# Products of probabilities and v, chunk by chunk on 64 rows and 32 columns of the array

## The chip, the cores and the metric

The kernel runs on one core of a Trainium2 chip. Its time is the device time of one execution in microseconds, given as the median of several; shorter is better. The core has TensorE (PE, matmuls into PSUM), VectorE (DVE), ScalarE (ACT), GpSimd (POOL) and SyncE (SP, which issues DMAs). They run side by side and wait for each other by semaphores.

## The reference

Two steps: attention by chunks, and a gated feed-forward network over all tokens. q, k and v are 4 x 8 heads x 768 tokens x 64, in float32. Each chunk of 32 queries sees 64 keys: 8 memory keys, 16 to its left, its own 32 and 8 to its right.

```
for c in range(nc):                                   # 24 chunks of 32
    k_full = concat([mem_k, k[l_start:r_end]])        # up to 64 keys
    v_full = concat([mem_v, v[l_start:r_end]])
    scores = scale * q_c @ k_full.T
    a = exp(scores - max(scores))
    a = a / (sum(a) + 1e-09)
    out[c] = a @ v_full
...
xn = x / sqrt(mean(x * x) + 1e-06) * rms_g            # x: 3072 tokens x 512
g, val = xn @ w_gate, xn @ w_val                      # 512 -> 1536
return (silu(g) * val) @ w_out                        # 1536 -> 512
```

## The kernel before

The 3072 tokens are 8 blocks of 384 tokens. A block's attention is 4 units of work, 32 in all, each two heads by 384 tokens, that is 12 chunks for each head. The feed-forward part of a block goes over 12 slices of 128 hidden columns; each slice has 12 matmuls `pg` (gate), 12 `pv` (value), both at L561, and 9 `po` (output) at L599. They work in a shortened float32 (fp32r) on values split into a high and a low part, so that each product is three matmuls.

Units 0 to 7 (two blocks) run at the start, in an order written out by hand as a string of tokens, while weights are still loaded and split. The other 24 units, of blocks 2 to 7, are put between the feed-forward matmuls of the block before: a generator puts the steps of its four units into the gaps between groups of matmuls, in six visits and one more for the norm. In visit n these are `stage_p` of unit n-1, `stage_s` of unit n, then `stage_o` and `stage_r` of unit n-2, and the steps after them. On TensorE everything of this later part stays in the order of the program (`on_pe`); the order of the other engines comes from a scheduler.

The steps of a unit that matter here:

- `stage_s` (L318) multiplies q and k: 12 matmuls in plain float32, one for each chunk, with 64 output rows (two heads x 32 queries) and 64 keys. The two heads' q lie block-diagonally in `qb` (`qp` in the late units), 128 x 64, so that one matmul over 128 rows (two heads x 64) does both heads.
- the maximum (L330), the difference (L336) and the exponential (L341) make `pe`.
- `stage_p` (L348) transposes `pe` into `pT`, three 128 x 128 blocks. In `pT` the partitions are keys: 64 of one chunk, 64 of the next.
- `stage_ch` (L227) copies `pT` into `pt` (late: a part of the tile `qp`), where each pair of chunks stands block-diagonally: rows 0 to 63 only in the columns of the first chunk of the pair (index cp = 0), rows 64 to 127 only in those of the second. The other places were set to zero once.
- `stage_o` (L368) multiplies `pt` by v. `vw` (late: `kv`) holds for each pair of chunks the 64 keys of one chunk on rows 0 to 63 and those of the other on rows 64 to 127, with a column of ones at the end that sums the probabilities. A matmul over 128 rows and 64 columns does a pair of chunks of one head: 65 moving columns, 12 matmuls a unit, into one bank of PSUM, `o`. The index par (0 or 1) puts the output on the partitions from 0 or from 64, and so on the left or right half of the array's columns.
- `stage_ra`, `stage_rb`, `stage_rc` (L382, L386, L391) divide by the sums into `x`.

`x` is then normed (L398, L411, L421), transposed into `xT` (L440) and split.

Of the kernel before, what the change touches and what calls it, by code (L numbers as in the profile page):

```python
# [17 lines left out]
B, H, S, D = 4, 8, 768, 64  # L18
NM = 8
CH = 32  # L20
# [47 lines left out]
def tile_kernel(ctx: ExitStack, tc: tile.TileContext, q, k, v, mem_k, mem_v,  # L68
                w_gate, w_val, w_out, rms_g, out):
    nc = tc.nc  # L70
# [35 lines left out]
    def on_pe(ins):  # L106
        if pinned:
            tc.keep_in_program_order(ins)

    def psum_a(name):  # L110
        return psa.tile([P, 512], F32, name=name, tag="at")

    def psum_m(tag, name):
        return psm.tile([P, 512], F32, name=name, tag=tag)
# [19 lines left out]
    def which(u):  # L134

        return 1 + u % 2 if u < NE else 0
# [223 lines left out]
    def stage_o(u):  # L360
        d = st[u]
        pt = pts[which(u)]
        o = psum_a(f"o{u}") if u >= NG else psum_m(f"o{1 + u % 2}", f"o{u}")
        for i in range(NT):
            for hh in range(2):
                for par in range(2):
                    c0 = (2 * i + hh) * (D + 1)
                    on_pe(nc.tensor.matmul(o[64 * par:64 * par + 64, c0:c0 + D + 1],  # L368
                                     lhsT=pt[:, i, 2 * par + hh].rearrange("p c q -> p (c q)"),
                                     rhs=d["v"][:, 2 * i + par, hh, :], start=True, stop=True))  # L370
        d["o"] = o

    def stage_r(u, x):
# [306 lines left out]
    for e in range(2):  # L680
        r = slice(64 * e, 64 * e + 64)
# [6 lines left out]
    def attn_visits(blk, x):  # L688


        us = list(range(blk * NG, (blk + 1) * NG))
        for n in range(NG + 2):
            with tc.high_priority():
                if 1 <= n <= NG:
                    stage_p(us[n - 1])
                if n < NG:
                    u = us[n]
                    stage_s(u)
                if n >= 2:
                    stage_o(us[n - 2])  # L700
                    stage_r(us[n - 2], x)
                if n < NG:
                    stage_m(u)
                    stage_e(u)
                if 1 <= n <= NG:
                    stage_c(us[n - 1])
                if n < NG and u + 1 < len(units):
                    stage_t(u + 1)
            if n >= 2 and us[n - 2] + 1 < len(units):
                load_v(us[n - 2] + 1)  # L710
            if n < NG and u + 2 < len(units):
                load_qk(u + 2)
            yield
        with tc.high_priority():
            stage_n(x)
        yield
# [75 lines left out]
    def tok_o(n):  # L792
# [12 lines left out]
        S=stage_s, M=stage_ma, a=stage_mb, E=stage_e, P=stage_p,  # L805
        C=lambda n, e="a": stage_ch(n, 0, e), m=lambda n, e="a": stage_ch(n, 1, e),
        O=stage_o, X=stage_ra, x=stage_rb, u=tok_u,

        N=tok_N, e=tok_e, Y=tok_Y, y=tok_y, z=tok_z, r=tok_r, A=tok_A, B=tok_B, D=tok_D,
# [119 lines left out]
```

## Time and profile before

| | before |
|---|---|
| median of 3 runs | 733.04 us (732.32 to 733.74) |
| the profiled execution, its own time | 731.54 us |
| its span on the core | 729.8 us |
| mean granted TensorE clock | 0.995 |
| matmul records of `o` in late units | 576 |
| matmul records of `s` in late units | 576 |

A line of the groups gives the line of the kernel, the engine and operation, the output and inputs by the program's names, the shape, how many, busy time and the mean of one in ns, and the idle time of the engine ahead of them with its cause. A matmul's shape reads rows*columns of the array that are in use, then partitions x elements of the moving operand. PE is TensorE's matmuls, PEld its weight loads. A line of the chain of waits gives the start, the length and what the program's end hung on in that time.

### The profile page before, as it was taken

To read this page: it belongs to the slowest core of one execution; us is meant where nothing else is said; L and a number is where in the kernel's file an instruction comes from. 1 tells how busy PE (TensorE), PEld (TensorE's weight loads), DVE (VectorE), ACT (ScalarE), POOL (GpSimd) and SP (SyncE) were. 2 spreads that over 40 slices of the span, in tenths; PEclk is the share of its full clock that TensorE was granted. 3 is DMA by queue.
4 is the path that set the end of the run, shared out by engine and by line. 5 is a ranking of instruction groups with operands and counts; after the bars stand their busy time and mean duration, and the time that the engine had idled before them with its cause. 6 is when DMAs were issued, how large, how long until landed. Compare 5 with 4: busy or idle time off the path is not lost.

```text
span 729.8 us, 13052 instructions
## 1 busy us (share of the span) xinstructions
PE 715.1 (98%) x5136; PEld 656.6 (90%) x5136; DVE 380.0 (52%) x725; ACT 287.8 (39%) x600; POOL 36.4 (5%) x143
## 2 busy tenths in 40 slices
PE   8889999999999999999999999999999999999997
PEld 7778999999989999899999999989998999999996
DVE  4888999865645443444535353445434543332222
ACT  4899676643452323422333232432234222341112
POOL 3300000001000000000000000000000000000000
PEclk8999999999999999999999999999999999999999
DMA  8994563414412320122212123021311210010001
GB/s 173 203 259 141 173 202 116 132 37 102 85 37 68 55 50 22 62 46 42 43 38 66 23 45 61 20 66 31 66 29 34 64 32 20 20 44 0 1 1 43
DMA packets 143173, 50.20 MB, mean 69 GB/s; under 512 B 126984, under 2 KB 134536, under 8 KB 143112
## 3 DMA queue, kind: packets, MB, share of 16 engines
q1 hardware_dynamic: 139832, 44.49, 26.6%
q10 hardware_dynamic: 3280, 4.88, 1.8%
q8 instruction: 40, 0.66, 0.4%
q14 instruction: 21, 0.17, 0.1%
HBM read 43.06 MB, written 6.29 MB: 68 GB/s over the span
## 4 chain that ended last, share of the span: by engine, by line
PE 92%; ACT 3%; DMA 3%; DVE 1%; issue 0%; POOL 0%; ACTq 0%; SPq 0%; POOLq 0%
PE pv L561 28%; PE po L599 28%; PE pg L561 27%; PE s L318 3%; PE o L368 3%; PE xT L440 1%; PE pT L348 1%; DMA ws<-in_moe_w_val_dram 1%; DMA memV<-in_mem_v_dram 1%; DMA vw<-in_v_dram 1%; ACT junk L398 0%; ACT ws L508 0%; ACT pt L227 0%; DMA kv<-in_v_dram 0%; ACT qb L227 0%
## 5 line engine op out<-in xcount | busy, mean ns | idle before, releaser
L561 PE MATMUL pv<-xh,wh_v 128*128 128x384 f32 x384 | 132.8, 346 | 0.0
L561 PE MATMUL pg<-xh,wh_g 128*128 128x384 f32 x384 | 129.7, 338 | 0.7 <-DVE t L572 0.7
L561 PE MATMUL pv<-xh,wl_v 128*128 128x384 f32 x384 | 129.5, 337 | 0.6 <-DVE wl_v L532 0.6
L561 PE MATMUL pg<-xh,wl_g 128*128 128x384 f32 x384 | 129.5, 337 | 0.0
L561 PE MATMUL pg<-xl,wh_g 128*128 128x384 f32 x384 | 129.3, 337 | 0.0
L561 PE MATMUL pv<-xl,wh_v 128*128 128x384 f32 x384 | 129.3, 337 | 0.0
L572 DVE SCALAR_TENSOR_TENSOR t<-t,pg 128x384 f32<-128x384 f32 x96 | 53.1, 553 | 138.6 <-ACT t L568 138.5
L227 ACT CAST hh<-t 128x384 fp32r<-128x384 f32 x95 | 48.7, 512 | 174.9 <-PE po L599 165.3
L599 PE MATMUL po<-wh_o,hh 128*128 128x512 f32 x285 | 113.8, 399 | 0.3
L599 PE MATMUL po<-wh_o,hl 128*128 128x512 f32 x285 | 113.1, 397 | 0.0
L599 PE MATMUL po<-wl_o,hh 128*128 128x512 f32 x285 | 112.1, 393 | 0.0
L584 DVE TENSOR_TENSOR hl<-t,hh 128x384 fp32r<-128x384 f32 x95 | 52.9, 557 | 100.7 <-ACT hh L227 95.7
L568 ACT ACTIVATE t<-pg 128x384 f32<-128x384 f32 x96 | 47.2, 492 | 135.9 <-PE pg L561 130.8
L575 DVE TENSOR_TENSOR t<-t,pv 128x384 f32<-128x384 f32 x95 | 52.5, 552 | 64.9 <-PE pv L561 64.4
L561 PEld LDWEIGHTS pg<-xh,wh_g 128*128 128x128 f32 x384 | 72.1, 188 | 4.4 <-DVE t L572 0.9
L561 PEld LDWEIGHTS pg<-xl,wh_g 128*128 128x128 f32 x384 | 72.1, 188 | 3.6
L561 PEld LDWEIGHTS pv<-xh,wh_v 128*128 128x128 f32 x384 | 72.1, 188 | 2.4
L561 PEld LDWEIGHTS pv<-xh,wl_v 128*128 128x128 f32 x384 | 72.2, 188 | 0.9 <-DVE wl_v L532 0.9
L561 PEld LDWEIGHTS pv<-xl,wh_v 128*128 128x128 f32 x384 | 72.2, 188 | 0.3
L561 PEld LDWEIGHTS pg<-xh,wl_g 128*128 128x128 f32 x384 | 72.1, 188 | 0.0
L599 PEld LDWEIGHTS po<-wh_o,hl 128*128 128x128 f32 x285 | 53.5, 188 | 14.1 <-DVE hl L584 1.8
L599 PEld LDWEIGHTS po<-wh_o,hh 128*128 128x128 f32 x285 | 53.5, 188 | 10.0 <-ACT hh L227 1.7
(112 smaller groups left out, 772.9 us busy)
## 6 DMA issues: line engine op xcount, KB each, us to landing
kn<-in_k_dram SPq DMA_DIRECT2D x96, 52.0 KB
qn<-in_q_dram SPq DMA_DIRECT2D x96, 48.0 KB
out_dram<-ob ACTq DMA_DIRECT2D x18, 256.0 KB
ws<-in_moe_w_gate_dram SPq DMA_DIRECT2D x4, 1024.0 KB
ws<-in_moe_w_val_dram SPq DMA_DIRECT2D x4, 1024.0 KB
ws<-in_moe_w_out_dram SPq DMA_DIRECT2D x4, 1024.0 KB
kv<-in_v_dram SPq DMA_DIRECT2D x48, 84.0 KB
kv<-in_v_dram SPq DMA_DIRECT2D x48, 70.0 KB
```

The lines of the kernel that those rows point to most:

```text
L227: return nc.scalar.copy(out, in_)
L318: on_pe(nc.tensor.matmul(s[64 * par:64 * par + 64, o:o + KC], lhsT=qb[:, c].rearrange("p s q -> p (s q)"), rhs=kw[:, c], start=True, stop= ...
L348: on_pe(nc.tensor.transpose(out=t[:, i * P:(i + 1) * P], in_=pe[:, i * P:(i + 1) * P], identity=ident))
L368: on_pe(nc.tensor.matmul(o[64 * par:64 * par + 64, c0:c0 + D + 1], lhsT=pt[:, i, 2 * par + hh].rearrange("p c q -> p (c q)"), rhs=d["v"][: ...
L440: on_pe(nc.tensor.transpose(out=t[:, i * P:(i + 1) * P], in_=tiles[i][:, kt * P:(kt + 1) * P], identity=ident))
L561: on_pe(nc.tensor.matmul(ps[:, 0:HT], lhsT=weight(a, n, f, kt), rhs=xs[c][:, kt], start=cnt == 0, stop=cnt == 3 * NKT - 1))
L568: nc.scalar.activation(t, g, AF.Tanh, scale=0.5)
L572: nc.vector.scalar_tensor_tensor(out=t, in0=t, scalar=1.0, in1=g, op0=ALU.add, op1=ALU.mult)
L575: nc.vector.tensor_tensor(out=t, in0=t, in1=vv, op=ALU.mult)
L584: nc.vector.tensor_tensor(out=hl, in0=t, in1=hh.bitcast(F32), op=ALU.subtract)
L599: on_pe(nc.tensor.matmul(po[i], lhsT=h[a][:, i * P:(i + 1) * P], rhs=weight(c, "o", f), start=f == 0 and n == 0, stop=f == NF - 1 and n == 2))
```

## The change

Only the loop in `stage_o` changes. Before, a matmul took the block-diagonal 128 x 64 of a pair of chunks and v of both chunks. Now each chunk has a matmul of its own: 64 rows (those of its chunk, index cp), 32 columns (its queries), the same 65 moving columns of v on those 64 rows. The output partitions are the same as before: 64 par + 32 cp. So each unit has 24 matmuls of 64 x 32 where it had 12 of 128 x 64. The zeros of `pt` are no longer read.

```diff
             for hh in range(2):
-                for par in range(2):
-                    c0 = (2 * i + hh) * (D + 1)
-                    on_pe(nc.tensor.matmul(o[64 * par:64 * par + 64, c0:c0 + D + 1],
-                                     lhsT=pt[:, i, 2 * par + hh].rearrange("p c q -> p (c q)"),
-                                     rhs=d["v"][:, 2 * i + par, hh, :], start=True, stop=True))
+                c0 = (2 * i + hh) * (D + 1)
+                for cp in range(2):
+                    for par in range(2):
+
+                        r, w = slice(64 * cp, 64 * cp + 64), 64 * par + 32 * cp
+                        on_pe(nc.tensor.matmul(o[w:w + CH, c0:c0 + D + 1], lhsT=pt[r, i, 2 * par + hh, cp],
+                                         rhs=d["v"][r, 2 * i + par, hh, :], start=True, stop=True))
```

On TensorE the groups keep their places. This is the third visit of block 3's attention, between two slices of block 2's feed-forward part; the shape is output rows x moving columns, and L561 is L563 after the change. Before:

```order
L561 MATMUL pg<-xh,wl_g_94 128x384
L348 MATMUL pT_2867<-ident,pe_2759 128x128 x3
L318 MATMUL s_2871<-kv,qp 64x64 x12
L368 MATMUL o_2884<-kv,qp 64x65 x12
L561 MATMUL pv<-xh,wh_v_95 128x384
```

And after:

```order
L563 MATMUL pg<-xh,wl_g_94 128x384
L348 MATMUL pT_3011<-ident,pe_2903 128x128 x3
L318 MATMUL s_3015<-kv,qp 64x64 x12
L371 MATMUL o_3028<-kv,qp 32x65 x24
L563 MATMUL pv<-xh,wh_v_95 128x384
```

Nothing moved; twelve products became 24. In each late block two of the four `o` groups stand right behind `s` like this one, one stands behind `pT` and one behind `pg`: 12, 6 and 6 of the 24 late groups. Of the early ones two stand right ahead of `s`.

On DVE, behind the same group, before:

```order
L382 TENSOR_SCALAR r_2897<-o_2884 128x6
L230 COPY qp<-pT_2867 64x12x32
L386 RECIPROCAL r_2897<-r_2897 128x6
L575 TENSOR_TENSOR t<-t,pv 128x384
L391 TENSOR_TENSOR x<-o_2884,r_2897 128x3x128
L584 TENSOR_TENSOR hl<-t,hh 128x384
```

And after (line numbers from L371 on are two higher):

```order
L384 TENSOR_SCALAR r_3053<-o_3028 128x6
L230 COPY qp<-pT_3011 64x12x32
L388 RECIPROCAL r_3053<-r_3053 128x6
L393 TENSOR_TENSOR x<-o_3028,r_3053 128x3x128
L577 TENSOR_TENSOR t<-t,pv 128x384
L586 TENSOR_TENSOR hl<-t,hh 128x384
```

The product `t` of the feed-forward part and the division into `x` changed places. This happens at 9 places of the late blocks, and at 6 the copy to `qp` comes to stand ahead of `x`; on ACT one tanh and the squares of block 2 change places. DMAs keep their order.

## The prediction

> **What bounds the kernel now.** First the page: who is busy, and who is on the chain that ended last.
>
> ```profile
> span 729.8 us, 13052 instructions
> ...
> PE 715.1 (98%) x5136; PEld 656.6 (90%) x5136; DVE 380.0 (52%) x725; ACT 287.8 (39%) x600; POOL 36.4 (5%) x143
> ...
> PE 92%; ACT 3%; DMA 3%; DVE 1%; issue 0%; POOL 0%; ACTq 0%; SPq 0%; POOLq 0%
> PE pv L561 28%; PE po L599 28%; PE pg L561 27%; PE s L318 3%; PE o L368 3%; PE xT L440 1%; PE pT L348 1%; DMA ws<-in_moe_w_val_dram 1%; DMA memV<-in_mem_v_dram 1%; DMA vw<-in_v_dram 1%; ACT junk L398 0%; ACT ws L508 0%; ACT pt L227 0%; DMA kv<-in_v_dram 0%; ACT qb L227 0%
> ```
>
> TensorE is busy for 98% and carries 92% of the chain; the changed line, `o` at L368, has 3% of it. A busy share says little of a pipelined engine, so I look at the stretches and then at the chain where it is not TensorE.
>
> ```profile
> 40.00:62.00 22.00, 18.63 (x231) 16.21 (x229) 19.12 (x38) 20.36 (x41) 0.33 (x1) 1.00 0.85 260
> 62.00:166.00 104.00, 104.00 (x552) 97.13 (x551) 90.56 (x135) 65.29 (x99) 2.23 (x6) 1.00 0.42 129
> 166.00:725.00 559.00, 557.67 (x3882) 512.50 (x3881) 244.50 (x495) 174.09 (x397) 20.93 (x85) 1.00 0.19 41
> ```
>
> The columns are the stretch, its length, then busy us (and instructions) of TensorE, its weight loads, DVE, ACT, POOL, and the granted clock (1.00). From 62 us on TensorE has no idle time to speak of: what it gets more to do there, the kernel gets longer by. Before 62 us it waits:
>
> ```profile
> 20.89 3.80 DMA vw<-in_v_dram
> ...
> 42.63 7.62 DMA ws<-in_moe_w_val_dram
> ...
> 59.83 1.24 DVE wl_v L532
> ...
> 61.10 2.02 PE pv L561 x10
> ```
>
> In this chain (start, us, what) transfers and the vector engines set the time until 61.10. The 8 early units (o groups between 21.7 and 56.8 us) lie there, so I cost them at nothing; without that cover each would cost what a late unit costs. The 24 late units (181 to 635 us) count in full.
>
> **What an o group costs now.** The timeline of TensorE: a matmul of plain f32 shows as two weight loads and two matmul records, so the 12 products of a unit are x24.
>
> ```profile
> 24.93 1.15 PE L307 MATMUL warm<-zero 128*64 128x64 f32 x16
> 26.12 0.28 PE L368 MATMUL o<-vw,pt 128*64 128x65 f32 x2
> ...
> 197.15 0.92 PE L368 MATMUL o<-kv,qp 128*64 128x65 f32 x24
> ```
>
> And all records of the line, with their least, median and longest ns, the first and last start:
>
> ```profile
> L368 PE MATMUL o<-kv,qp x576: 219/222/272, 181.1 to 635.6; 128*64 128x65 f32 x192
> ...
> L368 PE MATMUL o<-vw,pt x192: 219/222/272, 21.7 to 56.8; 128*64 128x65 f32 x192
> ```
>
> One record is 0.22 long and they overlap, so the starts of the 24 spread over 0.92 - 0.22 = 0.70 us: 30 ns apart. The filler `warm`, of nearly the same shape but always on the same 64 columns of the array, needs (1.15 - 0.22) / 15 = 62 ns. So the two column halves (par 0 and 1, in the outputs' rows 0 and 64) already run side by side, each with 12 pairs of 58 ns. The x2 row says the same: two records of at most 0.27 in 0.28, so the second started some 10 ns behind the first.
>
> Does a pair get shorter with narrower weights? Transposes show it, of 128 and 64 columns with the same 96 moving ones (at the lower clock of the start, both alike):
>
> ```profile
> 13.18 0.64 PE qT L237 x4
> 13.82 0.64 PE qT L240 x4
> ```
>
> No: moving columns set it, and these stay 65.
>
> **The change, part by part.** (1) Each unit issues 24 products instead of 12, x48 records, each on 64 rows and 32 columns: four places of the array, 12 pairs each, as many as each of the two places had. If the four run side by side as the two do now, the group still takes 12 x 58 ns = 0.70 us: price 0. No row shows two *row* halves at work, so the bounds are 0 and, if they take turns, another 12 x 58 ns = 0.70 us per unit. Below nothing I see no gain, since no place gets fewer pairs. I take 0: the column halves are the nearest row, and the four places, like those two, have no cell of the array in common.
>
> (2) The shape of the array's division. The scores `s` also use 128 rows and 64 columns. The chain of two visits in a late block, and the idle time before weight loads:
>
> ```profile
> 246.52 0.33 PE pT L348 x3
> 246.85 0.90 PE s L318 x24
> 247.75 0.70 PE o L368 x24
> 248.45 2.28 PE pv L561 x12
> 250.73 2.10 PE po L599 x9
> 252.82 2.11 PE pg L561 x12
> ...
> 275.98 0.33 PE pT L348 x3
> 276.31 0.85 PE o L368 x24
> 277.16 2.31 PE pv L561 x12
> ```
>
> ```profile
> 180.30 0.83 PEld L318 LDWEIGHTS s<-kv,qp 128*64 128x64 f32 x24 [0.17 <-issue]
> 181.00 0.84 PEld L368 LDWEIGHTS o<-kv,qp 128*64 128x64 f32 x24
> ```
>
> Behind the full-width transposes `pT` an o group costs 0.85; behind `s`, of its own shape, 0.70, and the weight load shows no idle time, where that of `s` behind `pT` shows 0.17 with nothing waited for. So passing from one division to another costs 0.15 us; I read it as the array running empty and the first weights loading uncovered. Back to full width costs 2.28 - 2.11 = 0.17 to 2.31 - 2.11 = 0.20. In the order of instructions 12 of the 24 late groups stand right behind `s`, 6 behind `pT`, 6 behind `pg`. After the change `s` and `o` differ, so those 12 pay an entry that they don't pay now. The price: 0.15 as the nearest row has it. Twice the columns cost 0.02 to 0.05 more (0.17 to 0.20 against 0.15), so half of them may cost 0.01 to 0.025 less: 0.125 to 0.14. That makes 12 x 0.125 to 12 x 0.15 = 1.5 to 1.8, and for the other groups, whose entry may shrink by as much, 0 to -0.3. Together 1.2 to 1.8; I take 1.5. The exits stay in number, and I leave them at their price.
>
> The Trainium skill, "TensorEngine Tiling (Array Packing)", Key Properties, has a rule that speaks against the change here: another mode of tiling, not merely another tile, drains the engine. By it the 12 added changes cost what the rows above say; were it wrong for 64x32 behind 128x64, the sum would be 0.
>
> (3) DVE's order. At 9 places, behind `o` groups that follow `s`, the scheduler now puts `x` ahead of the product `t` of L575, some 0.56 us later for `t`; at 6 others the copy to `qp` goes ahead of `x`.
>
> ```profile
> 251.44 0.56 DVE L575 TENSOR_TENSOR t<-t,pv 128x384 f32<-128x384 f32 x1
> 251.91 0.55 DVE L391 TENSOR_TENSOR x<-o,r 128x384 f32<-128x384 f32 x1
> ...
> 252.63 0.51 ACT L227 CAST hh<-t 128x384 fp32r<-128x384 f32 x1 [1.55 <-PE po L599]
> ```
>
> `t` ends at 252.00 and its reader waits until 252.63 for `po` to release `hh`; 0.56 later is 252.56, still covered. Without this cover it would be up to 0.56 at each of the 9, 5 us; but `hl`, which needs `hh`, and the bank of `pv` are asked for only a group or two of matmuls (2.1 us each) later. Price 0. One move on ACT (the squares of the first late block ahead of a tanh) has the same cover.
>
> **The sum.** The profiled execution took 731.54 (span 729.8), the median is 733.04, 1.5 more. On either base the change adds 0 + 1.5 + 0: **734.5** against the median, +0.2%, just at the 0.2% (1.5 us) that a measurement of this kernel can tell from no change.
>
> **Rivals.** *No drain between the two divisions* (12%): the passage costs nothing, since the column count alone may not make a division: the transposes above go from 128 to 64 columns without a pause. Against it: they are transposes, and every passage between matmuls of these two shapes pauses. Time 733.0, down to 732.7 with the smaller entries: not slower. It decides on whether the weight loads of the 12 groups show idle time.
>
> *The row halves take turns* (24%): both halves write the same bank, at different partitions, in one accumulator `o`, which two places in the same column half never do at once in any row here. Then a group takes 1.40 + entry: 24 x 0.70 = 16.8, with 1.5 for the entries 18.3: 751.3, and up to 24 x 0.70 + 8 x 0.70 more if the early units count. For it: no row shows row halves side by side. Against it: the places are disjoint in rows and columns. The Trainium skill, the same page, Gotcha 1, says that different row tiles cannot access one PSUM bank at the same time and that software must see to it; by that rule this rival holds, and no run here shows it yet.
>
> *Issue becomes the bound* (8%): 48 pairs in 0.70 us are one per 15 ns, and the closest lasting spacing that a row shows is 30 ns. With a floor halfway, 22 ns, a group takes 48 x 22 ns = 1.06: 24 x 0.36 + 1.5 = 10.1, or 743. Against it: the x2 row's starts 10 ns apart. The Trainium skill, "TensorE: Matmul & The Clock Gate", Wait — 56ns, not 53.3ns?, gives a floor of some 25 ns from start to start; by it the group would be an estimated 1.2 us and the kernel some 13 us longer.
>
> *All four one after another* (3%): 48 x 58 ns = 2.8, +50 us, 784.
>
> **How the numbers follow.** Forecast 53%, no drain 12%, turns 24%, issue 8%, all serial 3%. The likeliest is 734.5, by itself within 733.9 and 735.2. The range must reach to the turns to hold 8 in 10: 732.8 to 752. The forecast lies on the border of what can be told apart, so I split it: 28 slower, 25 within. No drain: 10 within, 2 faster. The others are slower. Faster 0.03 (with 1 for scatter), same 0.34, slower 0.63.
>
> **What would show it.** Right: the o groups x48 in a record length of about 0.92 as before; in the chain 0.82 to 0.85 for every o group, behind `s` too; idle time of about 0.17 before the weight loads of 12 more groups; pT, s, pg, pv, po unchanged. The turns: x48 over about 1.6. Issue: 1.2 to 1.4. No drain: 0.70 in the chain behind `s`. What would make it wrong beyond these: a pair on 64 rows that is longer or shorter than 58 ns, since every nanosecond of it counts 12 x 24 = 288 times, 0.3 us.

## The result and the profile after

The change makes the kernel slower by 0.65%. Measured side by side, the kernel before took 732.68 us (median of 4, 731.65 to 733.74) and the changed one 737.11 us (median of 4, 736.46 to 738.02): a ratio of 1.0065, 95% interval 1.0047 to 1.0083, or +4.4 us where +1.5 was forecast. The profiled execution took 737.38 us, 5.8 more than that of before (731.54). The places below are read from these two executions, so they have 1.4 us to share out that the medians don't show. The granted clock doesn't tell the two apart: each has one stretch of 8 us at a mean of 0.57 (12 to 20 us before, 10 to 18 us after) and 1.00 in the rest of the first 80 us.

The page after: the span, the busy time of the engines, the queue that brings the engines their instructions (packets, MB, share), and the chain by engine.

```profile
span 735.7 us, 14598 instructions
...
PE 717.4 (98%) x5904; PEld 656.9 (89%) x5904; DVE 380.4 (52%) x725; ACT 287.5 (39%) x600; POOL 36.2 (5%) x143
...
q8 instruction: 46, 0.75, 0.4%
...
PE 94%; ACT 2%; issue 1%; DVE 1%; DMA 0%; POOL 0%; SPq 0%; ACTq 0%; POOLq 0%
```

TensorE has 768 more matmul records and as many more weight loads, but is busy only 2.3 us longer. On the chain, transfers fell from 3% to nothing. So first the question where the time is. The late units' records of the changed line, with their first and last start, tell the two parts of the program apart:

```profile
L371 PE MATMUL o<-kv,qp x1152: 214/216/242, 185.5 to 641.1; 64*32 64x65 f32 x192
```

The first late group starts at 185.5, before at 181.1: **4.4 us are lost before any late unit.** From the first to the last it is 455.6 us, before 454.5: **1.1 us are lost in the late part**, the loss that the forecast was about. (The rest of the 5.8 lies behind 641.1 and is small.)

**The late part.** The chain over the same two visits as before:

```profile
251.35 0.90 PE s L318 x24
252.25 0.82 PE o L371 x48
...
280.73 0.33 PE pT L348 x3
281.06 0.82 PE o L371 x48
281.88 2.31 PE pv L563 x12
```

The group behind `s` costs 0.82 instead of 0.70, and the one behind `pT` 0.82 instead of 0.85. The 6 groups behind `pg` gain the same 0.03 in the starts of TensorE's records. So with 12 of the first kind and 12 of the other: 12 x 0.12 - 12 x 0.03 = 1.1 us, just what the two starts give. The timeline of the same `s` and `o`, matmuls and weight loads:

```profile
251.28 0.97 PE L318 MATMUL s<-kv,qp 128*64 128x64 f32 x24
252.18 0.89 PE L371 MATMUL o<-kv,qp 64*32 64x65 f32 x48
```

```profile
251.28 0.83 PEld L318 LDWEIGHTS s<-kv,qp 128*64 128x64 f32 x24 [0.17 <-issue]
252.18 0.72 PEld L371 LDWEIGHTS o<-kv,qp 64*32 64x32 f32 x48
```

48 records of 0.22 in 0.89 us: their starts spread over 0.67, one per 14 ns, where 24 spread over 0.70. So the four places work side by side. The passage shows only in part as idle time of the weight loads: those of `s` end at 251.28 + 0.83 = 252.11, those of `o` begin at 252.18, 0.07 later. More of it shows in the starts: the loads of `o` begin 0.90 behind those of `s`, before 181.00 - 180.30 = 0.70 behind them, and of these 0.20 us 0.12 are left in the chain.

**The early part.** The timeline has four places at which TensorE stands still and waits for nothing that the profile shows:

```profile
28.38 0.66 PE L371 MATMUL o<-vw,pt 64*32 64x65 f32 x32 [0.75 <-issue]
...
35.35 0.30 PE L237 MATMUL qT<-ident,qf 96*128 96x96 f32 x1 [1.28 <-issue]
...
54.58 1.44 PE L371 MATMUL o<-vw,pt 64*32 64x65 f32 x83 [1.37 <-issue]
...
61.57 0.66 PE L371 MATMUL o<-vw,pt 64*32 64x65 f32 x31 [0.49 <-issue]
```

0.75 + 1.28 + 1.37 + 0.49 = 3.9 us, and all four stand on the chain. They are most of the 4.4; where the rest comes from stays open. Three of the four cut an `o` group in two; one stands before a transpose, so it isn't the group's own. How many records TensorE had done when each began is what a stretch from the start to the pause counts:

```profile
0.00:27.42 27.42, 22.89 (x345) 20.54 (x345) 14.75 (x33) 15.06 (x32) 9.69 (x47) 0.88 0.96 182
0.00:33.84 33.84, 27.54 (x471) 24.56 (x471) 19.98 (x45) 19.46 (x44) 11.83 (x51) 0.90 0.98 187
0.00:53.00 53.00, 42.71 (x718) 37.05 (x719) 34.54 (x76) 35.61 (x80) 12.71 (x52) 0.94 0.98 200
0.00:60.87 60.87, 49.21 (x845) 43.04 (x845) 41.09 (x86) 41.86 (x93) 12.71 (x52) 0.94 0.92 198
```

Matmuls and loads together: 690, 942, 1437, 1690 records. They lie 252, 495 and 253 apart: one step of about 250, twice that step, and one step again. The queue of instructions has such a step too. Before, its row was

```profile
q8 instruction: 40, 0.66, 0.4%
```

and 6 packets more came for 2 x 768 = 1536 more records: 256 to a packet. (The other kernels fit: 42 packets for 384 more records in experiment 1, 51 for 2880 in experiment 8.) The records leave out the engine's semaphore and register instructions, so a packet of 256 instructions holds a few less than 256 of them. Counted with those instructions, 705, 961, 1473 and 1729 lie ahead of the four pauses in the trace: exactly 256, 512 and 256 apart.

The pauses are TensorE reaching the end of the instructions that have arrived. The trace has the packets of the instruction queue with their times, and each pause ends 1.3 to 1.7 us after one of them has landed:

| packet of the queue, start to landing | TensorE goes on |
|---|---|
| 25.27 to 26.67 | 28.38 |
| 32.38 to 33.88 | 35.35 |
| 52.20 to 53.31 | 54.58 |
| 59.15 to 60.17 | 61.57 |

In all ten kernels profiled here, TensorE begins none of these steps of 256 less than 1.2 us after the landing of its packet. In the kernel before, it begins none less than 4 us after, and there are no such pauses.

What the pauses do to the end is told by the chain, at the place where the transfer of `ws` carried it for 7.62 us before:

```profile
52.01 0.84 PE warm L307 x12
52.85 0.35 PE o L371 x13
53.20 1.37 issue
54.58 1.44 PE o L371 x83
```

No transfer of data is left there. The engines, held up, had become later than the transfers that used to cover them.

### The profile page after: what moved, and what is told of

It is laid out like the page before. It is cut to its first block, busy times and chain, and to the rows that moved or that the text cites. A ratio compares the mean times of both kernels' runs of the same rounds, so it can differ in the third digit from the quotient of the medians.

```text
span 735.7 us, 14598 instructions
## 1 busy us (share of the span) xinstructions
PE 717.4 (98%) x5904; PEld 656.9 (89%) x5904; DVE 380.4 (52%) x725; ACT 287.5 (39%) x600; POOL 36.2 (5%) x143
## 4 chain that ended last, share of the span: by engine, by line
PE 94%; ACT 2%; issue 1%; DVE 1%; DMA 0%; POOL 0%; SPq 0%; ACTq 0%; POOLq 0%
PE pv L563 28%; PE po L601 27%; PE pg L563 27%; PE s L318 4%; PE o L371 3%; PE xT L442 1%; PE pT L348 1%; PE pm L307 1%; ACT qb L227 0%; DVE kw L230 0%; ACT pt L227 0%; DMA kv<-in_v_dram 0%; PE po L629 0%; PE qT L237 0%; ACT wy L511 0%
## 5 line engine op out<-in xcount | busy, mean ns | idle before, releaser
L563 PE MATMUL pv<-xh,wh_v 128*128 128x384 f32 x384 | 132.8, 346 | 0.0
L563 PE MATMUL pg<-xh,wh_g 128*128 128x384 f32 x384 | 129.6, 338 | 0.7 <-DVE t L574 0.7
L563 PE MATMUL pg<-xh,wl_g 128*128 128x384 f32 x384 | 129.5, 337 | 0.0
L563 PE MATMUL pv<-xh,wl_v 128*128 128x384 f32 x384 | 129.4, 337 | 0.0
L563 PE MATMUL pg<-xl,wh_g 128*128 128x384 f32 x384 | 129.3, 337 | 0.0
L563 PE MATMUL pv<-xl,wh_v 128*128 128x384 f32 x384 | 129.3, 337 | 0.0
L563 PEld LDWEIGHTS pg<-xh,wh_g 128*128 128x128 f32 x384 | 72.1, 188 | 4.4 <-DVE t L574 0.9
L563 PEld LDWEIGHTS pg<-xl,wh_g 128*128 128x128 f32 x384 | 72.1, 188 | 3.7
L563 PEld LDWEIGHTS pv<-xh,wh_v 128*128 128x128 f32 x384 | 72.1, 188 | 3.0
L563 PEld LDWEIGHTS pv<-xl,wh_v 128*128 128x128 f32 x384 | 72.2, 188 | 0.3
L563 PEld LDWEIGHTS pv<-xh,wl_v 128*128 128x128 f32 x384 | 72.2, 188 | 0.0
L563 PEld LDWEIGHTS pg<-xh,wl_g 128*128 128x128 f32 x384 | 72.1, 188 | 0.0
```

The costliest lines, as they stand in the source:

```text
L563: on_pe(nc.tensor.matmul(ps[:, 0:HT], lhsT=weight(a, n, f, kt), rhs=xs[c][:, kt], start=cnt == 0, stop=cnt == 3 * NKT - 1))
```

## The experiments

Each kernel was timed in the same session as the kernel before; the ratios are against that.

**1 and 2: the two parts apart.** The new loop for the early units alone, and for the late ones alone (there the condition is `u >= NE`; NE is 8, the number of early units).

```diff
+                if u < NE:
+                    for cp in range(2):
...
+                else:
+                    for par in range(2):
...
```

> The change in the 8 early units alone; the 24 late ones keep 12 products of 128 rows and 64 columns. Theory 1 (instructions arrive late): the early part alone carries most of the loss, 2.5 to 4 us over the kernel before, as three or four pauses of 0.7 to 1.5 us that wait for nothing in the profile, some 256 TensorE records (or a multiple) apart, and the late part keeps its length. Theory 2 (passages between divisions are all, the rest is scatter between executions): 0 to 0.5 us over the kernel before, no such pauses.

> The change in the 24 late units alone. Theory 1: 12 passages at 0.12 less 12 shorter entries at 0.03, so 0.9 to 1.6 us over the kernel before, with a chain of 0.82 for every late o group. Theory 2: the whole 4.4 us.

The early units alone: 736.32 against 732.72, ratio 1.0045 (1.0027 to 1.0062), +3.6. The late ones alone: 734.30 against 732.72, 1.0026 (1.0015 to 1.0037), +1.6. (The interval of the second is 1.1 to 2.7 us. Together the two make 5.2 where the whole change made 4.4; their intervals allow for that.) The stretches of the first, up to each of its pauses (1.17, 0.74 and 0.65 us long):

```profile
0.00:25.00 25.00, 20.30 (x345) 18.12 (x345) 15.14 (x33) 15.04 (x32) 9.54 (x47) 1.00 0.94 181
0.00:31.83 31.83, 24.94 (x471) 22.14 (x471) 20.35 (x45) 19.45 (x44) 11.68 (x51) 1.00 0.96 185
0.00:52.75 52.75, 40.74 (x718) 35.21 (x719) 35.63 (x76) 35.67 (x80) 12.55 (x52) 0.99 0.98 200
```

In time they begin up to 2.4 us earlier than in the changed kernel, in records at exactly the same 690, 942 and 1437. The fourth is missing: there the packet had landed 3.2 us before it was needed. The late groups of this kernel run as in the kernel before, 454.7 us from the first start to the last (186.2 to 640.9). The other kernel has one such pause, of 0.70 us up to 51.85, but there the chain hangs on the transfer of `ws` until 51.85 anyway. Its late part is 638.5 - 182.8 = 455.7 long, +1.2:

```profile
L372 PE MATMUL o<-kv,qp x1152: 213/216/242, 182.8 to 638.5; 64*32 64x65 f32 x192
```

So both losses are real and lie where the trace has them. Kernels with the old early units start their late part at 181.1 to 183.7 (six of them, counting the kernel before), those with the new ones or with as many records at 185.5 to 187.8, but for the kernel of experiment 7 (182.7): the 4.4 of one pair is good to some 2 us, and the +3.6 of the medians is the better figure. The granted clock may have a share in these starts: in the profiles of experiments 1, 3, 5 and 6 it falls to some 0.5 for 3 to 8 us between 50 and 60 us, in those of the kernel before and the changed one it doesn't.

**3: late scores in the same division.** If the passage from 128 x 64 to 64 x 32 is what costs in the late part, it goes away when `s` is divided alike.

```diff
+            if u < NE:
...
+                continue
+            for hh in range(2):
+                r, w = slice(64 * hh, 64 * hh + 64), 64 * par + 32 * hh
+                on_pe(nc.tensor.matmul(s[w:w + CH, o:o + KC], lhsT=qb[r, c, hh], rhs=kw[r, c], start=True, stop=True))
```

with the late `o` of experiment 2.

> In the late units the scores too are taken by head, on 64 rows and 32 columns, so that s and o have the same division; early units as before. If the passage between unlike divisions is the late cost: no idle time before the weight loads of the 12 groups behind s, those groups 0.68 to 0.70 in the chain, entries of all groups 0.03 shorter, and in sum 0.5 to 1.2 us less than the kernel before. If the cost lies in products on 64 rows and 32 columns themselves: the 12 groups stay at 0.82, and the s groups get longer too, 1 to 3 us over the kernel before.

730.69 against 732.72, ratio 0.9972 (0.9959 to 0.9985): this version takes 0.3% less than the kernel before. Its chain:

```profile
248.17 0.33 PE pT L353 x3
248.50 0.83 PE s L324 x48
249.32 0.69 PE o L377 x48
...
277.78 0.82 PE o L377 x48
```

Behind `s` the passage is gone (0.69), elsewhere it stays (0.82). `s` itself went from 0.90 to 0.83. By block, four `s` save 0.07, two `o` behind `s` 0.01 and two others 0.03: 0.36, for six blocks 2.2 us. The late part is 452.5 us long (183.2 to 635.7), 2.0 less than before. It is more than the 0.5 to 1.2 that I expected, since I had given `s` only the cheaper passage of 0.03; where its other 0.04 come from, no run separates.

**4: late scores alone.** The same edit of `s`, with the old `o`: now the two are unlike the other way round.

> Only the late scores by head on 64 rows and 32 columns; o as before, early units as before. If any unlike neighbours pay the passage: the 12 o groups behind s cost 0.85 instead of 0.70 (12 x 0.15 = 1.8), while the 24 s groups gain 0.07 each as where both were changed (-1.7): within 0.7 us of the kernel before. If only the passage into the narrow division costs: o behind s stays at 0.70, and the kernel gains 1.4 to 2 us.

732.62 against 732.04, ratio 1.0002 (0.9988 to 1.0016): no difference.

```profile
247.44 0.83 PE s L324 x48
248.26 0.85 PE o L373 x24
```

`s` gains its 0.07, and the 128 x 64 group behind it now pays 0.85 for 0.70. 24 x -0.07 + 12 x 0.15 = +0.1; the late part shows +0.3 (181.7 to 636.5, 454.8). The passage costs in both directions, and experiment 3 gains by the pair.

**5: columns alone.** Late `o` with 128 rows and 32 columns: half as many columns, all the rows, the zeros of `pt` read again.

```diff
+                            w = 64 * par + 32 * cp
+                            on_pe(nc.tensor.matmul(o[w:w + CH, c0:c0 + D + 1], lhsT=pt[:, i, 2 * par + hh, cp],
+                                             rhs=d["v"][:, 2 * i + par, hh, :], start=True, stop=True))
```

> Late units: 24 products on all 128 rows (the block-diagonal half with its zeros read again) and 32 columns; early units as before. If the column count alone makes a division: the 12 groups behind s show 0.17 us of idle time before their weight loads and cost 0.82, and the time is that of the late change alone, 0.9 to 1.6 us over the kernel before. If it takes the split of the rows: no idle time there, 0.70, and the kernel before within 0.5 us. In both, 0.70 us for 48 records would show that four column places run side by side.

733.61 against 732.72, ratio 1.0016 (1.0006 to 1.0027).

```profile
249.56 0.90 PE s L318 x24
250.45 0.82 PE o L371 x48
```

The same 0.82: going from 64 to 32 columns with the same rows is a passage already. (The idle time of 0.17 that I expected before the weight loads shows as 0.06 only, much as in the changed kernel.) The late part is 455.5 long, +1.0 where the row halves have +1.1 and +1.2. So nothing of the late loss comes from two row halves that write one bank.

**6: products that are nearly empty.** Are the early pauses the work of the narrow products, or only of their number? The kernel before, with one more matmul behind each early product: the same weights of 128 x 64, but one moving column, into a place of `o` that nobody reads. This adds work.

```diff
                                      rhs=d["v"][:, 2 * i + par, hh, :], start=True, stop=True))
+                    if u < NE:
+                        nc.tensor.matmul(o[64 * par:64 * par + 64, 400:401],
+                                         lhsT=pt[:, i, 2 * par + hh].rearrange("p c q -> p (c q)"),
+                                         rhs=d["v"][:, 2 * i + par, hh, 0:1], start=True, stop=True)
```

> The kernel before, with a second product of one moving column behind each product of the 8 early units, into a free column of the same bank: as many TensorE records as the change makes there, but on 128 rows and 64 columns; late units as before. Theory 1: the same pauses at records near 690, 942 and 1437, and 2 to 4 us over the kernel before. If the pauses come from the narrow products: none at those records, and 0 to 1 us over the kernel before.

736.99 against 732.04, ratio 1.0066 (1.0044 to 1.0088), +5.0, more than the 2 to 4 that I expected. Up to its pauses (0.46, 0.59 and 1.21 us long):

```profile
0.00:27.81 27.81, 22.28 (x344) 20.24 (x345) 15.14 (x33) 15.26 (x32) 9.64 (x47) 0.94 0.93 187
0.00:34.27 34.27, 27.98 (x470) 25.59 (x470) 19.97 (x45) 19.35 (x43) 11.77 (x51) 0.95 0.95 189
0.00:52.89 52.89, 43.89 (x717) 38.98 (x717) 34.76 (x76) 35.65 (x81) 12.65 (x52) 0.97 0.96 205
```

689, 940 and 1434 records: the same places within 3, though no product has 64 rows or 32 columns. In whole instructions they are again 705, 961 and 1473. The number of instructions makes the pauses, not the array's division. (Its late part, 187.8 to 642.2, is 454.4 long.)

**7: the count shifted.** If the pauses belong to numbers in the stream, 64 more records in front move them to earlier work. In the order of the early part, 16 products of the filler `warm` go ahead of an `s`; they add work that nobody reads.

```diff
-K0a Q1a S0 p2
+K0a Q1a W16 S0 p2
```

> The changed kernel with 16 more filler matmuls (64 TensorE records) put where TensorE waits 2.5 us anyway, ahead of the first scores. In the changed kernel the pauses fell behind TensorE records 690, 942, 1437 and 1690, weight loads and matmuls counted from the start. Theory 1 (instructions are fetched in blocks of 256 and arrive late): they stay at those record numbers to within about 10, and so move 64 records back in the program, out of the third o group into the transposes and fillers ahead of it; some may vanish or appear, and the time changes by up to 3 us either way. If the pauses belong to the new products themselves (an operand or a place of the array that is late): they stay at the same products and show at 754, 1006, 1501, 1754, the time within 1 us of the changed kernel's.

734.10 against 732.04, ratio 1.0026 (1.0008 to 1.0043): with *more* work, no more is left of the change than the late loss (experiment 2: 1.0026). The pauses at 690 and 942 are gone. A third is at

```profile
0.00:46.49 46.49, 38.58 (x719) 33.66 (x720) 30.89 (x68) 32.06 (x74) 12.86 (x52) 1.00 0.97 192
```

1439 records, where the changed kernel had it at 1437; had it stayed with its product it would be at some 1437 + 64 = 1501. In whole instructions it is 1473 in both. The pause now falls into filler, 0.55 us ahead of a transpose:

```profile
48.50 0.33 PE L307 MATMUL warm<-zero 128*64 128x64 f32 x3 [1.81 <-issue]
49.05 0.52 PE L348 MATMUL pT<-ident,pe 128*128 128x128 f32 x3 [0.21 <-DVE r L388]
```

In the kernel before TensorE waits at that place anyway:

```profile
48.67 0.52 PE L348 MATMUL pT<-ident,pe 128*128 128x128 f32 x3 [1.26 <-DVE r L386]
```

so the transpose comes 49.05 - 48.67 = 0.4 later for a pause of 1.8, and the chain hangs on the transfer of `ws` again:

```profile
43.21 8.64 DMA ws<-in_moe_w_val_dram
```

The first late group starts at 182.7. The first two pauses are gone and not moved because the packets of these two steps had landed 3.1 and 1.6 us before they were needed. But the gain need not be all theirs. In this profile the granted clock is 1.00 through the first 80 us, where the changed kernel has 8 us at 0.57; and the two of its ten executions with the lowest mean clock (0.995) took 735.96 and 737.30, about as long as the changed kernel's four (736.46 to 738.02, clock 0.988 to 0.995). The pauses themselves don't need the lower clock, since experiment 1 has two of them before 50 us at 1.00; but no run holds the clock and moves the steps, so how much of the 3.0 us is theirs stays open.

**8: dense records in the late part.** The late `o` groups have 96 records each, loads included, between groups of 9 to 12 long matmuls, and show no pause. Is it that they are too few in a row, or that the late part's transfers are light? In experiment 2's kernel the products of the first unit of each late block are issued four times over: 384 records at a stretch, at six places, the same result written each time.

```diff
-        for i in range(NT):
+        for i in list(range(NT)) * (4 if u >= NE and u % 4 == 0 else 1):
```

> The change in the late units alone, and in the first unit of each late block the 24 products are issued four times over (the same values again): 384 TensorE records in a row at the spacing of the changed groups, in a part of the run where the DMA engines are little loaded. Repeating costs 6 x 3 x 0.7 = 12 to 13 us over the late change alone. If dense records alone outrun the supply of instructions: in most of these six groups a pause of 0.5 us or more that waits for nothing, and 15 to 20 us over the late change alone. If it takes the loaded DMA engines of the first 60 us as well: no pause in them, each group 2.7 to 2.9 us long, and 12 to 13 us.

749.69 against 732.65, ratio 1.0232 (1.0215 to 1.0249); against experiment 2 it is +15.4, of which the repeats are 6 x 3 x 0.69 = 12.4. The time lies in the range of the first expectation (15 to 20), but neither came true as I had put it, "most" or "none" of the six: two groups are cut, and one more pause, of 1.48 us, stands behind a third group (before a matmul at 434.76) and is put down to DVE. The two that are cut:

```profile
340.40 2.37 PE L372 MATMUL o<-kv,qp 64*32 64x65 f32 x150
343.92 0.84 PE L372 MATMUL o<-kv,qp 64*32 64x65 f32 x42 [1.15 <-issue]
...
608.90 2.35 PE L372 MATMUL o<-kv,qp 64*32 64x65 f32 x147
611.87 0.88 PE L372 MATMUL o<-kv,qp 64*32 64x65 f32 x45 [0.61 <-issue]
```

and the records up to the three pauses:

```profile
0.00:342.56 342.56, 329.50 (x3135) 301.42 (x3136) 219.85 (x399) 169.27 (x334) 24.51 (x97) 1.00 0.43 105
0.00:433.07 433.07, 418.82 (x4029) 383.34 (x4029) 259.67 (x479) 197.56 (x399) 27.97 (x111) 1.00 0.38 92
0.00:611.04 611.04, 595.23 (x5688) 545.21 (x5688) 337.57 (x636) 253.17 (x526) 34.94 (x139) 1.00 0.33 78
```

6271, 8058 and 11376 records, 1787 = 7 x 255.3 and 3318 = 13 x 255.2 apart: the same step as in the early part, at the pause put down to DVE too. In whole instructions they are 6337, 8129 and 11457, that is 705 + 22, 29 and 42 x 256, and all three end 1.4 to 1.5 us behind the landing of a packet (342.55, 433.38, 610.41): the packet explains that one without the DVE. The three make 1.15 + 1.48 + 0.61 = 3.2 us, and with the 12.4 of the repeats 15.6, near the 15.4 measured. Around the last the DMA engines are idle:

```profile
608.70:612.70 4.00, 3.39 (x202) 3.06 (x198) 2.83 (x6) 0.94 (x3) 0.40 (x2) 1.00 0.01 4
```

A share of 0.01, and from 609.4 to 611.8 the packet of instructions is the only one:

```profile
DMA packets 1, 0.02 MB, mean 7 GB/s; under 512 B 0, under 2 KB 0, under 8 KB 0
...
q8 instruction: 1, 0.02, 2.4%
```

So a pause needs no loaded DMA. Three of the six stretches went through without any, and the trace shows the difference: in the three with a pause a whole step of 256 lies inside the stretch, in the others it doesn't. Here the packet of the next step starts 0.3 to 1.2 us behind a step's first record and lands some 0.95 later, and such a step takes 2.7 to 3.5 us from its first record to the next step's. In the changed kernel's early part the packets of the four pauses start 2.2 to 6.2 us behind and take 1.0 to 1.5, and the steps take 5.3 to 8.6 us, other waits included. So the supply is slower there; that the loaded DMA engines make it so is likely, but no run changes the load alone.

## Why the prediction was right, and where it failed

- **Slower, and by little: right.** 737.11 lies within the range; but of +4.4 only a quarter is what the sum held, and the forecast's own 733.9 to 735.2 was missed. The range reaches as far as 752 for the sake of the row halves taking turns, which did not happen. That it held the pauses too is luck.
- **(1) Four places side by side, price 0: right.** 48 starts in 0.67 us. The rival that the row halves take turns (1.40 a group) fell with it, and so did the issue floor (halfway at 22 ns): records start 14 ns apart on four places. (The x2 row that I set against it could not tell: with records of 0.22 to 0.27 in 0.28 us, the second starts anywhere from 10 to 60 ns behind the first.) The Trainium skill's sentence in "TensorEngine Tiling (Array Packing)", Gotcha 1, that row tiles can't reach one PSUM bank at the same time, isn't borne out by this case: the two row halves write one bank, at different partitions, in the same 0.82 us as four places over all rows (experiment 5). Nor is the floor of some 25 ns from start to start that the Trainium skill gives in "TensorE: Matmul & The Clock Gate", Wait — 56ns, not 53.3ns?; across places the starts are closer, 14 ns.
- **(2) The passage between divisions: right in kind, a little too dear.** Forecast 1.2 to 1.8, taken as 1.5; measured 1.1 in the changed kernel, 1.2 in experiment 2 by the trace. The added passage was 0.12 for the 0.15 taken, the smaller entry elsewhere 0.03 for the 0.025. I took the row of the wide matmuls as it stood, and the estimate for narrow ones would have been the better choice. "No drain" fell: experiments 3 and 5 show that a passage is paid where the division changes, columns alone sufficing, and not where it stays. (That it is the array running empty is an argument; the runs show its price.)
- **(3) The moves on DVE and ACT, price 0: right.** The late part holds the 1.1 of the groups and no more.
- **The step that failed: "so I cost them at nothing".** I had said what an early group would cost without its cover: "what a late unit costs", 0.1 or so. But it is not the group that got longer. The early part holds eight groups that went from 48 to 96 records, among short transposes, scores and filler; its stream of records became denser than its instructions arrive, and TensorE stood still four times, 0.5 to 1.4 us each. That is +3.6 by experiment 1, and the cover of some transfers wasn't long enough for it. I had the number of records in the change's first sentence, and priced only what they do in the array. That the engine ran out of instructions is shown twice over: by the steps of exactly 256 (experiments 1, 6, 7 and 8) and by the packets of the instruction queue, 1.2 to 1.7 us after whose landing each pause ends.
- **The signs.** x48 in about 0.92 (0.89) and 0.82 to 0.85 in the chain came as said. Idle time of about 0.17 ahead of 12 more weight loads didn't: only 0.07 of the passage shows there. The start of a group against the start of the one before is the better sign.

## What to carry to other kernels

Splitting a matmul into more, smaller ones costs nothing in the array as long as the places lie side by side, but it costs a passage of 0.12 to 0.15 us wherever the neighbour on TensorE is divided otherwise: divide the neighbours alike (experiment 3, the fastest here). And it costs instructions: where hundreds of short records follow each other, count them, and look for idle time with no cause at steps of 256 of the engine's instructions (some 250 records), just behind a packet of the instruction queue. A step that TensorE works off in some 2 us (256 records at the late groups' 96 in 0.7 us) is faster than its supply, which took 2.7 us or more wherever TensorE had caught up with it. A stretch that is covered by transfers has a cover of a certain length only; ask how much more the engines may take before they, not the transfers, are late.

## What was not expected of the hardware

- TensorE pauses of 0.46 to 1.48 us (1.8 in filler), which the profile puts down to no releaser but once, come at the same number of records in kernels with different work: 690 and 690 and 689; 942, 942, 940; 1437, 1437, 1439, 1434; in whole instructions always at 705 plus a multiple of 256. Each ends 1.2 to 1.7 us after a packet of the instruction queue has landed. More work in front removes them or moves them onto other work.
- Matmul records on four disjoint places start 14 ns apart, on 64 x 32 and on 128 x 32 alike, where two places have 30 ns and one 62.
- Scores cut into 64 x 32 cost 0.83 for 0.90 us, with the same moving columns and 48 records for 24.
